# An S4D convolution with a gated MLP: inverse transform of unsummed products, a skip term on TensorE, and a tabled order of work

## The chip, the cores and the metric

One core of a Trainium2 chip. Its engines run side by side, each with a queue of its own that is worked off in order: PE (TensorE: matrix products into PSUM, with PEld its weight loads), DVE (VectorE), ACT (ScalarE), POOL (GpSimd) and SP, which here only issues DMAs. The metric is device time in microseconds (us); the kernel before took 973.34 us in the median of three runs (969.08 to 975.69). Lower is better.

## The reference, cut to what matters

```python
def A(u):                                  # L 2048, D 640, N 128
    K = 2 * einsum("dn,dnl->dl", C * dt, exp(A * dt * pos)).real
    y = irfft(rfft(K, 2 * L) * rfft(u, 2 * L))[:, :L]     # per channel
    return y + u * D_skip
def B(x):                                  # F 1728
    return (silu(x @ w1) * (x @ w3)) @ w2
sa, ca, ga, sb, cb, gb = silu(c) @ w_mod
x = x + ga * A(layernorm(x) * (1 + ca) + sa)
x = x + gb * B(layernorm(x) * (1 + cb) + sb)
```

All data is float32. A matrix product of plain float32 is two records in the trace.

## The kernel before, in words

**Stages.** The first 400 us or so compute A, the rest B (`ffn`, L1412), which the change leaves alone. A goes over five blocks of 128 channels; each block has the same steps, and steps of up to three blocks are under way at one time. Tasks have names with the block in front, and the trace has the names of the tiles:

- *Kernel chunks*, `g{b}.{c}`, eight per block (`gen_chunk` L594, `gen_tasks` L1739). POOL makes the phases (`ph`) and three products of exponentials (`z0` to `z2`, into the tiles yy and xx), ACT five sines and cosines (`s0` to `s4`, tile tr), DVE five products (`m0` to `m4`, yy and xx), PE 32 products into a PSUM tile kps (`p`, 64 records), ACT copies kps to ks (`r`), and DVE adds the skip term D_skip to one column of ks (`d`, `skip` L1761). Tiles ph, xx and yy have two buffers each; kps is one PSUM bank, used half by half.
- *h*, `h{b}.{i}`, four per block (`h_tasks` L1793): load x (`l`), normalise (`n`, four instructions, on ACT or DVE), two DVE steps (`x`, `a`; tiles hn and hb), store (`o`), and one fetch in another layout into xb (`h{b}.f`).
- *Row products*, `hh{b}.{i}` from xb and `k{b}.{i}` from ks, eight each (`first_tasks` L1812): PE (`m`, PSUM tile ps), then a copy to the spectrum sp (`e`, on ACT or DVE).
- *Spectra*, `w{b}.{i}`, eight per block (`spectra_tasks` L1851): PE makes the spectrum of h (`f`, tile fh) and of the kernel (`k`, tile fk), ACT copies the first to SBUF (`h`, tile hz). Their complex product is four real products and two sums. DVE makes two products into the tile fp (`x0`), two in place in PSUM (`x1`), and then the subtraction and the addition (`c`, two instructions of 256 elements, `both` L1879). Two such i are one *inverse* on PE (`z{b}.{j}`, `inverse` L1886, tile fz, weights wz): two products for each half of the partitions, real and imaginary part. It is copied to zt (`v0`, `v1`) and stored to zd (`o0`, `o1`).
- *Tail* (`tail_tasks` L1073): zd is read back (iz, and izb for the last block), a last set of products and an add make the new x, and its layernorm (`xn`), transposes (`tp`) and first weights lead into B.

Before all that `early_tasks` (L2000) loads x, the parameters and w_mod, makes the parameters' polar form (`pa`, `pb`, `pc`, `q`), the layernorm's statistics (`hscale`) and the modulation (`mr`, `mc`, `fold`, `cols`).

**Order.** Every step is a task of a class `Plan`: engine or two engines to choose from, a length, what it comes after, and the buffers it takes and gives. `place` (L188) walks the tasks with a model of the five engines (lengths, lags, DMA rate) and picks at each point the one that can start first, ranks breaking ties. The 1520 ranks in RANKS (L34) come from a search. The tasks are issued in that order (L270), so it is the order of every engine's queue.

Of the kernel before, what the change touches and what calls it, by code (L numbers as in the profile page):

```python
# [29 lines left out]
EXPS = ((0, 0, 0, 64.0), (0, 1, 0, 1.0), (1, 0, 0, 512.0), (1, 1, 4, 8.0), (1, 2, 0, 8.0))  # L30
# [2145 lines left out]
```

## Time and profile before

| what | value |
|---|---|
| median of three runs | 973.34 us |
| the profiled execution | 972.31 us |
| its span, first to last instruction | 970.5 us |
| mean granted TensorE clock | 0.975 |
| A, to the first product of B | 0 to 398 us |
| B | 398 to 970.5 us |

Times in the profile count from the start of the span. A group's line names line, engine, operation, output<-inputs, shape and count; then busy time, mean length in ns, and the idle time of the engine right before these instructions with what ended it. Most lines read L157, the helper through which tasks are issued, so groups go by tile names. Lengths of neighbouring DVE instructions overlap by some 0.08 us; from start to start is what the queue pays.

### The profile page before, as it was taken

Reading aid. Unit: us, or ns where it says so; the run is one execution under the profiler, and the core shown is the slowest. Engines: PE = TensorE matmul, PEld = TensorE weight load, DVE = VectorE, ACT = ScalarE, POOL = GpSimd, SP = SyncE. Lnnn points to the kernel's source line nnn. Section 1 sums busy time; section 2 is a strip of 40 time slices with the busy share of each in tenths; the row PEclk is TensorE's granted clock in tenths of the full one; section 3 lists DMA queues with packets and bytes.
Section 4 is the critical chain, followed back from the end, with each engine's and each line's share of the span. In section 5 each row is a group of like instructions: output and inputs, shape, how many; then the busy total and the mean of one; then the engine's idle time right before and its main releaser. Section 6 shows DMA issues by size and latency. Waiting matters only on the chain.

```text
span 970.5 us, 20551 instructions
## 1 busy us (share of the span) xinstructions
PE 859.9 (89%) x7985; PEld 681.8 (70%) x7985; DVE 702.0 (72%) x1395; ACT 546.4 (56%) x1022; POOL 340.5 (35%) x371
## 2 busy tenths in 40 slices
PE   1464787889899997899999999999999999999997
PEld 1132665767778884677777778888788888888775
DVE  7998899999999968886767677557456464645422
ACT  6877788979888851564434455346444344443412
POOL 1797889879799600002111111000011212120000
PEclk9996999999999999799999999999999999999999
DMA  9955453723425268935434422276342322220374
GB/s 218 275 168 191 111 136 95 177 66 106 111 80 152 74 159 206 241 118 182 122 120 139 122 96 68 82 209 194 112 134 64 102 77 86 82 82 28 108 220 133
DMA packets 110506, 127.31 MB, mean 131 GB/s; under 512 B 10568, under 2 KB 90696, under 8 KB 109128
## 3 DMA queue, kind: packets, MB, share of 16 engines
q1 hardware_dynamic: 109032, 125.21, 45.3%
q8 instruction: 63, 1.03, 0.5%
q10 hardware_dynamic: 1376, 0.79, 0.3%
q14 instruction: 35, 0.29, 0.1%
HBM read 95.82 MB, written 30.15 MB: 130 GB/s over the span
## 4 chain that ended last, share of the span: by engine, by line
PE 70%; DVE 17%; ACT 5%; issue 4%; DMA 3%; POOL 1%; SPq 1%; ACTq 0%; DVEq 0%
PE c L157 19%; PE acc L157 18%; PE X L157 12%; PE ps L157 4%; PE gu L157 3%; DVE yy L157 3%; PE kps L157 3%; PE fz L157 2%; PE fk L157 2%; DVE fp L157 2%; PE fh L157 2%; DVE hn L157 2%; DVE xx L157 2%; DVE xb L157 1%; ACT tr L157 1%
## 5 line engine op out<-in xcount | busy, mean ns | idle before, releaser
L157 PE MATMUL acc<-ah,w 128*128 128x512 f32 x560 | 173.2, 395 | 2.4 <-DMA w<-w2d 1.7
L157 PEld LDWEIGHTS acc<-ah,w 128*128 128x128 f32 x560 | 103.7, 188 | 26.4 <-issue 2.1
L157 PE MATMUL acc<-al,w 128*128 128x512 f32 x260 | 102.4, 394 | 0.0
L665 DVE TENSOR_TENSOR wl<-s,wh 128x256 fp32r<-128x256 f32 x92 | 38.9, 423 | 67.5 <-ACT wh L664 67.1
L841 POOL TENSOR_TENSOR s<-wr 128x256 f32<-128x256 f32 x22 | 16.4, 744 | 187.8 <-DMA wr<-in_w 94.8
L157 POOL TENSOR_TENSOR ph<-p,p 128x1024 int32<-128x1024 int32 x40 | 79.2, 1979 | 8.2 <-ACT tr L157 8.0
L664 ACT ACTIVATE wh<-s 128x256 fp32r<-128x256 f32 x92 | 37.6, 410 | 78.5 <-PE X L157 58.1
L157 PE MATMUL kps<-yy,xx 128*32 128x64 f32 x2560 | 51.8, 234 | 28.6 <-DVE xx L157 21.4
L157 DVE TENSOR_TENSOR yy<-yy,tr 128x512 f32<-128x512 f32 (+1 forms) x80 | 75.3, 943 | 1.2 <-ACT tr L157 0.6
L157 PEld LDWEIGHTS kps<-yy,xx 128*32 128x32 f32 x2560 | 45.1, 116 | 38.3 <-issue 22.0
L664 ACT ACTIVATE wh<-wr 128x256 fp32r<-128x256 f32 x92 | 38.4, 418 | 56.0 <-PE X L157 42.3
L842 POOL TENSOR_TENSOR s<-s,wr 128x256 f32<-128x256 f32 x22 | 16.6, 755 | 134.0 <-issue 133.9
L902 ACT ACTIVATE t<-g 128x512 f32<-128x512 f32 x44 | 27.8, 632 | 52.7 <-DVE g L866 52.7
L157 ACT ACTIVATE tr<-ph,hpi 128x512 f32<-128x512 f32 x80 | 54.6, 690 | 4.4 <-DVE xx L157 2.7
L157 PEld LDWEIGHTS acc<-al,w 128*128 128x128 f32 x260 | 48.9, 188 | 10.8 <-DVE al L665 0.3
L871 DVE SCALAR_TENSOR_TENSOR g<-t,g 128x512 f32<-128x512 f32 x48 | 33.7, 702 | 31.3 <-ACT t L902 29.3
L157 POOL TENSOR_TENSOR yy<-e,e 128x512 f32<-128x512 f32 x48 | 52.4, 1109 | 8.8 <-PE kps L157 5.9
L157 DVE TENSOR_TENSOR xx<-tr,xx 128x512 f32<-128x512 f32 x80 | 54.3, 680 | 1.1 <-ACT tr L157 1.1
L157 PE MATMUL ps<-wk,ks 128*64 128x128 f32 x640 | 42.4, 285 | 13.6 <-DVE ks L157 8.9
L157 ACT ACTIVATE tr<-ph 128x512 f32<-128x512 int32 x80 | 47.3, 598 | 12.4 <-DVE yy L157 6.5
L157 PE MATMUL ps<-wk,xb 128*64 128x128 f32 x640 | 46.1, 295 | 6.3 <-ACT sp L157 3.0
L157 PEld LDWEIGHTS ps<-wk,ks 128*64 128x64 f32 x640 | 37.0, 143 | 20.3 <-ACT hn L157 6.6
(448 smaller groups left out, 2379.7 us busy)
## 6 DMA issues: line engine op xcount, KB each, us to landing
w<-w2d SPq DMA_DIRECT2D x42, 640.0 KB, 3.9
wr<-in_w SPq DMA_DIRECT2D x50, 320.0 KB, 3.9
zd<-zt SPq DMA_DIRECT2D x40, 256.0 KB, 2.9
w2d<-w SPq DMA_DIRECT2D x14, 640.0 KB, 3.5
xs<-in_x SPq DMA_DIRECT2D x16, 320.0 KB, 11.3
hs<-hb SPq DMA_DIRECT2D x20, 256.0 KB, 2.5
xb<-hs SPq DMA_DIRECT2D x20, 256.0 KB, 4.9
iz<-zd SPq DMA_DIRECT2D x32, 160.0 KB, 5.0
```

Source lines behind the costliest of these rows:

```text
L157: self.prev = self.k.order(f(*a, **kw), self.prev)
L664: self.nc.scalar.activation(H, v, AF.Copy)
L665: eng.tensor_tensor(Lo, v, H.bitcast(F32), op=ALU.subtract)
L841: eng.tensor_tensor(s[0], u[:, 0:2], u[:, 2:4], op=ALU.add)
L842: eng.tensor_tensor(s[1], s[0], g[:, 0:2], op=ALU.subtract)
L871: V.scalar_tensor_tensor(g, th, 1.0, g, op0=ALU.add, op1=ALU.mult)
L902: tanh = lambda o, i: A.activation(o, i, AF.Tanh, scale=0.5)
```

## The change

**Unsummed products.** A constant FORM = "AABBB" gives each block a form. Blocks 2 to 4 (B) work as before. In blocks 0 and 1 (A) one DVE instruction of 1024 elements makes all four real products into an fp tile of twice the size, nothing is summed on DVE, and PE's inverse takes four products for each half in place of two, with a third set of weights (minus the first), so that PSUM makes the sums. The spectra's PSUM layout changes from (q r d) to (r q d).

**Skip term.** The DVE task `d` is gone. PE adds D_skip to kps: four products of 32x32 weights (a part of the identity) with four columns, accumulated behind the chunk's 32 products. kps becomes one tile of half a bank with one buffer.

**Third yy buffer.** In blocks 0 to 3 each third chunk takes its yy in the memory of x2[0], which is loaded later for that.

**Smaller edits.** al8, the input of the exponents, is built inside the table of exponentials. All row products of block 0 but k0.0 to k0.3 use the four rotating PSUM banks instead of three. The first two loads of zd in the tail go to the memory of a spectrum instead of a pool that opens later. Lengths of tasks are changed, which nothing reads any more.

**Order.** `place`, its model and RANKS are gone. A table ORDER of 1686 numbers gives the order: each is a task's place in the order in which tasks are added, and a tick (') means the second of its two engines. By it, among others:

- 8 of h's 20 norms are on DVE (13 before), 28 of 80 spectrum copies (20 before), 8 of 40 copies of zt (9 before).
- DVE, behind fold, up to the last add of h in block 0: h0.3.x g0.4.m0 h0.3.a g0.3.m4 g0.4.m1 h0.0.x h0.0.a h0.1.x g0.4.m2 g0.4.m3 h0.1.a g0.4.m4 h0.2.n t1.0.3 h0.2.x h0.2.a.
- DVE, from chunk 7 of block 0: g0.7.m4 h1.2.x g1.0.m0 h1.2.a g1.0.m1 hh0.0.e g1.0.m2 h1.0.x h1.0.a g1.0.m3 g1.0.m4 g1.1.m0 g1.1.m2 k0.6.e.
- PE around it: hh0.3.m hh0.7.m hh0.1.m g0.6.p hh0.5.m hh0.2.m hh0.0.m g0.7.p hh0.6.m hh0.4.m k0.7.m k0.5.m k0.6.m g1.0.p w0.0.f w0.0.k. Before: g0.7.p k0.7.m hh0.0.m g1.0.p hh0.1.m hh0.3.m hh0.2.m hh0.4.m hh0.5.m hh0.6.m hh0.7.m g1.1.p w0.0.f.
- SP: h0.f h1.1.l h1.2.l h1.0.l wb h1.1.o. Before: c1 c2 wb c3 h0.0.o h0.1.o h0.2.o c4 h0.3.o h0.f.

```diff
-RANKS = """
+ORDER = """
+1 80 78 81 79 82 83 150' 2 4 19 42 20 41 14 21 15 84 22 43 23 44 16 85 151 24 17 25 26 45 46 18 28 59 47 30 27 29 48 96 33 36 49
...
+FORM = "AABBB"
...
-    wz = np.tile(np.stack([np.block([c, s]), np.block([-s, c])], 1), (2, 1, 1))
+    wz = np.tile(np.stack([np.block([c, s]), np.block([-s, c]), np.block([-c, -s])], 1), (2, 1, 1))
...
+    def sequence(self):
...
+        for x in ORDER.split():
+            n = names[int(x.rstrip("'"))]
...
+            out.append((engs[x.endswith("'")], n))
...
+    def in_third(self, b, c):
+        return b < NB - 1 and (8 * b + c) % 3 == 2
+
+    def third(self):
+        return self.x2[0].rearrange("p j d -> p (j d)")[:, :2048].rearrange("p (r d a i) -> p r d a i", r=2, d=self.CD, a=2)
...
-        yy = w.tile([P, 2, C, 2, 32], F32, name=f"yy_{d0}", tag="yy")
+        yy = self.third() if self.in_third(d0 // P, d0 % P // C) else w.tile([P, 2, C, 2, 32], F32, name=f"yy_{d0}", tag="yy")
...
+            for q in range(4):
+                g = slice(32 * q, 32 * q + 32)
+                nc.tensor.matmul(kps.rearrange("p (e b) -> p e b", b=64)[g, :, 63], self.ident[g, g], self.dsk[g, d0 // P, d0 % P // 4:d0 % P // 4 + 4],
+                                 start=False, stop=True, skip_group_check=True, tile_position=(32 * q, 32 * q))
...
-                if b == c == 0:
-                    self.kg = self.psg.tile([P, 2, 256], F32, name="kps", tag="kg", bufs=1)
-                kps[c] = self.kg[:, c % 2]
+                kps[c] = self.psg.tile([P, 256], F32, name=f"kps{b}{c}", tag="kg", bufs=1)
...
-        def skip(c):
-            o = slice(4 * c, 4 * c + 4)
-            V.tensor_add(self.ks[b][:, o, 63], kps.pop(c).rearrange("p (e b) -> p e b", b=64)[:, :, 63], self.dsk[:, b, o])
...
-            to = k if r else prod[i // 2][:, :, i % 2 * 2:i % 2 * 2 + 2, :].rearrange("p r q d -> p q r d")
-            nc.vector.tensor_mul(to, k, bc(held[i][:, :, r], 2, 2))
+            k = bank.pop((1, i)).rearrange("p q r d -> p r (q d)")
+            h = held[i].rearrange("p q r d -> p r (q d)")
+            to = prod[i // 2][:, :, :, o, :].rearrange("p s r q d -> p s r (q d)")
+            nc.vector.tensor_mul(to, bc(k, 1, 2), bc(h, 2, 2))
...
-            for r in range(2):
+            for n, (s, r, w) in enumerate(((0, 0, 0), (0, 1, 1), (1, 1, 2), (1, 0, 1))[:2 if last else 4]):
                 for f in range(2):
                     g = slice(64 * f, 64 * f + 64)
-                    nc.tensor.matmul(bank["z", j, f], self.wz[g, r, :], p[g, r], start=(r == 0), stop=(r == 1), tile_position=(64 * f, 0))
+                    nc.tensor.matmul(bank["z", j, f], self.wz[g, w, :], p[g, s, r], start=(n == 0), stop=(n == (1 if last else 3)), tile_position=(64 * f, 0))
...
-            if b == 0:
-                x[0] = self.ks[0].rearrange("p e b -> p (e b)")[:, :1024]
...
+            x[0] = E[0][:, :, 1, :]
...
-            if u < 3:
-                z[u] = [self.ip.tile([P, 2, 512], F32, name=f"iz{u}{pr}", tag=f"iz{pr}", bufs=3) for pr in range(2)]
...
+            s = self.sp2.rearrange("p a b c -> p (a b c)")
+            t = s[:, :2048] if u == 0 else s[:, 2048:] if u == 1 else self.xb if u == 3 else self.ip.tile([P, 2048], F32, name="iz2")
```

More of the change, by code (lines that the diff above doesn't have):

```diff
@@ L28 @@
 HB2 = P // 2
[L30 removed]
+EXPS = ((0, 0, 0, 64.0), (1, 0, 0, 512.0), (1, 1, 4, 8.0), (1, 2, 0, 8.0), (0, 1, 0, 1.0))
 LOADS = 20
@@ L168 @@
 class Plan:
-    LAG = dict(PE=0.2, DVE=0.18, ACT=0.2, POOL=0.15, SP=0.0)
-    CHAIN = dict(DVE=0.12, ACT=0.12, POOL=0.07)
-    NEAR, RATE, LAND, FLY, ISSUE, AWAY, TABLE = 0.1, 235e3, 1.3, 0.7, 0.06, 8, 1.28
     def __init__(self, **rings):
@@ L258, in place @@
+        taken, done, out = {r: [] for r in self.n}, set(), []
+        for x in ORDER.split():
+            n = names[int(x.rstrip("'"))]
+            engs, _, _, after, _, _, take, give, _, _ = T[n]
+            assert n not in done and done.issuperset(after), n
+            for r, y, _ in take:
+                i = len(taken[r]) - self.n[r]
+                assert i < 0 or not uses[r, taken[r][i]], n
+                taken[r].append(y)
             for k in give:
                 uses[k] -= 1
-                given[k] = max(fin + self.LAG.get(e, 0.0), given.get(k, 0.0))
@@ L261, in place @@
-                if not uses[k]:
-                    freed[k] = given[k]
-            for m in nexts[n]:
-                left[m] -= 1
-                if not left[m]:
-                    ready.append(m)
-        assert len(end) == len(T), ("never", [n for n in T if n not in end][:20])
-        return order
-    def run(self):
-        T = self.tasks
-        found = [int(x) for x in RANKS.split()]
-        searched = [n for n in T if n not in self.own]
-        assert len(found) == len(searched)
-        self.order = self.place({n: t[4] for n, t in T.items()} | dict(zip(searched, found)))
-        for s, f, e, n in self.order:
-            if T[n][2]:
-                T[n][2](e)
+            done.add(n)
@@ L282 @@
+            out.append((engs[x.endswith("'")], n))
+        assert len(done) == len(T)
+        return out
+    def run(self):
+        for e, n in self.sequence():
+            if self.tasks[n][2]:
+                self.tasks[n][2](e)
 class K:
@@ L1113, in dst @@
                         return z[u][pr][h * 64:h * 64 + 64]
-                    load(f"iz{u}.{pr}{h}", zv[:, t0:t0 + 2, :cut], dst, 262144, done + ([f"hh{b4}.{i}.m" for i in range(8)] if u > 2 else []))
+                    load(f"iz{u}.{pr}{h}", zv[:, t0:t0 + 2, :cut], dst, 262144, done + ([f"hh{b4}.{i}.m" for i in range(8)] if u > 2 else []),
+                         "inv" if u < 2 else "change")
         def load_up(m):
@@ L1169, in lo @@
                     self.low(h[:, :k], l[:, :k], x)
-                add(f"wh{m}.{i}", "ACT", .36, hi, names + (after[i:i + 1] if after else []), rank)
-                add(f"wl{m}.{i}", "DVE", .42, lo, [f"wh{m}.{i}"], rank)
+                add(f"wh{m}.{i}", "ACT", .32, hi, names + (after[i:i + 1] if after else []), rank)
+                add(f"wl{m}.{i}", "DVE", .34, lo, [f"wh{m}.{i}"], rank)
         def down_split(m, rank):
@@ L1175, in hi @@
                 w2[m] = self.w2_high(m, w2r[m])
-            add(f"w2h{m}", "ACT", .73, hi, [f"ld{m}.{i}" for i in range(1 if m < 13 else 2)], rank, take=[("w2", 1)])
-            add(f"w2l{m}", "DVE", .82, lambda: self.w2_low(m, w2r[m], w2[m]), [f"w2h{m}"] + (["ln1"] if m in (0, 13) else []), rank)
+            add(f"w2h{m}", "ACT", .66, hi, [f"ld{m}.{i}" for i in range(1 if m < 13 else 2)], rank, take=[("w2", 1)])
+            add(f"w2l{m}", "DVE", .74, lambda: self.w2_low(m, w2r[m], w2[m]), [f"w2h{m}"] + (["ln1"] if m in (0, 13) else []), rank)
             add(f"w2k{m}", "SP", 0, lambda: self.w2_keep(m, w2[m]), [f"w2l{m}", "izb1"], rank, dma=[655360],
@@ L1237, in prepare @@
             add(f"iyb{b}", "PE", 1.9, lambda: last_inv(b), [f"izb{b}", f"lwd{b}", "border"] + (["iyb0"] if b else []), 16.0, take=[("gu", 1)])
-            add(f"iab{b}", "DVE", .7, lambda: last_plus(b), [f"iyb{b}"] + [f"lx{b}.{q}" for q in range(4)], rank, give=[("gu", f"iyb{b}"), ("w2", f"izb{b}")])
-            add(f"isb{b}", "DVE", 1.15, lambda: last_stats(b), [f"iab{b}"], rank)
+            add(f"iab{b}", "DVE", .6, lambda: last_plus(b), [f"iyb{b}"] + [f"lx{b}.{q}" for q in range(4)], rank, give=[("gu", f"iyb{b}"), ("w2", f"izb{b}")])
+            add(f"isb{b}", "DVE", .78, lambda: last_stats(b), [f"iab{b}"], rank)
             steps = {}
@@ L1267, in lo @@
                     self.low(*self.x_of(X, b, k), v[b, k])
-                add(f"tp{b}.{k}", "PE", .88, tp, [f"xn{b}.{j}" for j in range(4)] + [f"tp{b}.{k - 1}"] * (k > 0) + ([f"ia{4 + j}" for j in range(4)] + ["iab1"] if b else []), r - b)
-                add(f"v{b}.{k}", ("ACT", "DVE"), (.77, .81), shift, [f"tp{b}.{k}"], r, take=[("tmp", 1)] if k == 4 else [])
-                add(f"xh{b}.{k}", "ACT", .6, hi, [f"v{b}.{k}"], r)
-                add(f"xl{b}.{k}", "DVE", .69, lo, [f"xh{b}.{k}"], r, give=[("tmp", f"v{b}.{k}")] if k == 4 else [])
+                add(f"tp{b}.{k}", "PE", .6, tp, [f"xn{b}.{j}" for j in range(4)] + [f"tp{b}.{k - 1}"] * (k > 0) + ([f"ia{4 + j}" for j in range(4)] + ["iab1"] if b else []), r - b)
+                add(f"v{b}.{k}", ("ACT", "DVE"), (.7, .74), shift, [f"tp{b}.{k}"], r, take=[("tmp", 1)] if k == 4 else [])
+                add(f"xh{b}.{k}", "ACT", .54, hi, [f"v{b}.{k}"], r)
+                add(f"xl{b}.{k}", "DVE", .6, lo, [f"xh{b}.{k}"], r, give=[("tmp", f"v{b}.{k}")] if k == 4 else [])
         prepare(0, 16)
@@ L1587, in inv @@
             self.sp2 = self.fpool.tile([P, 16, P, 2], F32, name="sp2")
-        plan.add("inv", None, 0, inv, ["cols", "mag1"], 0)
+        plan.add("inv", None, 0, inv, ["cols", "mag1", "hscalef", "colsf", "q0.v1", "q1.v1"] + [f"h0.{i}.a" for i in range(4)] + [f"k0.{i}.e" for i in range(4)] +
+                 [f"rw{g}" for g in range(4)], 0)
         self.early_tasks(e)
@@ L1613, in border @@
             self.x2 += [self.fp.tile([P, 4, D], F32, name=f"x2{i}") for i in (2, 3)]
-        plan.add("change", None, 0, change, [f"g{b}.7.p", f"g{b}.7.d"] + [f"h{b}.{i}.x" for i in range(4)], 0, own=True)
+        plan.add("change", None, 0, change, [f"g{b}.7.p", f"g{b}.7.r"] + [f"h{b}.{i}.x" for i in range(4)], 0, own=True)
         self.tail_tasks(border, cut)
@@ L1787, in gen_tasks @@
                     give=[("tr", n + f"s{(0, 0, 1, 3, 4)[i]}")])
-            add(n + "p", "PE", 1.1, lambda c=c: ch[c][4](), [n + f"m{i}" for i in range(5)], t + 3,
-                take=[("kg", 1)], give=[("yy", n + "z0"), ("xx", n + "z2")])
+            add(n + "p", "PE", 1.3, lambda c=c: ch[c][4](), [n + f"m{i}" for i in range(5)] + (["dsk"] if b == 0 else []), t + 3,
+                take=[("kg", 1)], give=[(yy, n + "z0"), ("xx", n + "z2")])
             add(n + "r", "ACT", .27, lambda c=c: rows(c), [n + "p"] + ([f"k{b - 1}.{i}.m" for i in range(8)] if b else ["exp0", "q0.t0", "q1.t0"]), t + 3, give=[("kg", n + "p")])
-            add(n + "d", "DVE", .1, lambda c=c: skip(c), [n + "r"] + (["dsk"] if b == 0 else []), t + 3, give=[("kg", n + "p")])
     def h_tasks(self, b):
@@ L1803, in h_tasks @@
             place = (lambda: self.pbank("hn")) if b else (lambda: self.psg.tile([P, 512], F32, name="hn", tag="f", bufs=3))
-            add(n + "n", ("ACT", "DVE"), (1.95, .85), lambda e, i=i, place=place: self.h_norm(b, i, place(), e), [n + "l", "hscale"], t, take=[(bank, 1)],
+            add(n + "n", ("ACT", "DVE"), (1.89, 1.66), lambda e, i=i, place=place: self.h_norm(b, i, place(), e), [n + "l", "hscale"], t, take=[(bank, 1)],
                 give=[("xq", n + "l")] if b else [])
@@ L1925, in spectra_tasks @@
             j = i // 2
+            y = "c" if last else "x"
             n = f"z{b}.{j}."
-            add(n + "z", "PE", 1.95, lambda j=j: inverse(j), [f"w{b}.{i - 1}.c", f"w{b}.{i}.c"], t + W["late"], take=[("bank", 1), ("bank", 1, "'")],
-                give=[("fp", f"w{b}.{i - 1}.x0")])
+            add(n + "z", "PE", 1.92 if last else 3.86, lambda j=j: inverse(j), [f"w{b}.{i - 1}.{y}", f"w{b}.{i}.{y}"], t + W["late"], take=[("bank", 1), ("bank", 1, "'")],
+                give=[("fp", f"w{b}.{i - 1}.x")])
             for f in range(2):
@@ L1951, in exps @@
                 A.activation(E[t][:, :, m, :], x[0][:, :, k:k + n], AF.Exp, scale=-s)
-        add(f"al8{b}", ("POOL", "DVE"), (1.9, 1.13), begin, [f"al{min(b, 1)}"] + (["inv"] if b > 1 else []) + ([f"exp{b - 1}"] if b > 1 else ["turn1"] if b else []), t, port=True,
-            take=[("xs", 1)] if b == 1 else [])
-        add(f"exp{b}", "ACT", 3.46, exps, [f"al8{b}"] + ([f"g{b - 2}.7.z{i}" for i in range(3)] if b > 1 else ["turn1"] if b else []), t, table="exp",
-            give=[("xs", f"al8{b}")] if b == 1 else [])
+        add(f"al8{b}", ("POOL", "DVE"), (1.9, 1.13), begin, [f"al{min(b, 1)}"] + ([f"exp{b - 1}"] + [f"g{b - 2}.{c}.z{i}" for c in (5, 6, 7) for i in range(3)] if b > 1 else ["turn1"] if b else []), t, port=True)
+        add(f"exp{b}", "ACT", 3.46, exps, [f"al8{b}"], t, table="exp")
         add(f"mag{b}", ("POOL", "DVE"), (1.07, .62), lambda e: self.eng(e).tensor_tensor(E[1][:, :, 0], E[1][:, :, 0], bc(self.mag[:, b], 2, 4), op=ALU.mult),
@@ L2071, in early_tasks @@
             for j in range(4):
-                add(f"su{b}{j}", "ACT", .85, lambda b=b, j=j: st[b][0](j), [f"x{b}"], t + .01 * j)
-                add(f"sq{b}{j}", "ACT", .9, lambda b=b, j=j: st[b][2](j), [f"mean{b}"], t + .05 + .01 * j, give=[("xs", f"x{b}")])
+                add(f"su{b}{j}", "ACT", .74, lambda b=b, j=j: st[b][0](j), [f"x{b}"], t + .01 * j)
+                add(f"sq{b}{j}", "ACT", .83, lambda b=b, j=j: st[b][2](j), [f"mean{b}"], t + .05 + .01 * j, give=[("xs", f"x{b}")])
             add(f"mean{b}", "DVE", .1, lambda b=b: st[b][1](), [f"su{b}{j}" for j in range(4)], t, port=True)
@@ L2086, in scale @@
             self.h_rs = self.rsqrt(self.gp, self.h_ss, NJ, "h", (self.h_nm, 1.0), 1.0 / D, [t[:, i * NJ:(i + 1) * NJ] for i in range(2)])
-        add("hscale", "DVE", 6.5, scale, [f"mean{b}" for b in range(4)] + [f"sq{b}{j}" for b in range(4) if b not in W["stat_v"] for j in range(4)], W["stat"](4), take=[("f2", 1)])
+        add("hscale", "DVE", 5.5, scale, [f"mean{b}" for b in range(4)] + [f"sq{b}{j}" for b in range(4) if b not in W["stat_v"] for j in range(4)], W["stat"](4), take=[("f2", 1)])
         add("hscalef", None, 0, None, ["hscale"], give=[("f2", "hscale")])
@@ L2095, in rows_begin @@
             A.activation(m[:96, 384:], pm[0][:96, 384:], AF.Copy)
-        add("m", "ACT", .9, rows_begin, ["mr4"], 20, take=[("hz", 4)])
+        add("m", "ACT", .6, rows_begin, ["mr4"], 20, take=[("hz", 4)])
         pr = {}
@@ L2111, in early_tasks @@
             add(f"pr{g}", "PE", .9, lambda g=g: spread(g), ["m"], 21, take=[("f2", 1)], give=[("hz", "m")])
-            add(f"rw{g}", "ACT", .8, lambda g=g: keep(g), [f"pr{g}", "lat1", "pa4"], 21, give=[("f2", f"pr{g}")])
+            add(f"rw{g}", "ACT", .55, lambda g=g: keep(g), [f"pr{g}", "lat1", "pa4"], 21, give=[("f2", f"pr{g}")])
         def fold():
@@ L2117, in fold @@
             V.tensor_mul(self.rB, self.rB, self.rows[2])
-        add("fold", "DVE", 1.6, fold, [f"rw{g}" for g in range(4)], 22, port=True)
+        add("fold", "DVE", 3.2, fold, [f"rw{g}" for g in range(4)], 22, port=True)
         add("wb", "SP", 0, lambda: nc.sync.dma_start(self.wb, self.t_wb), ["fold", "mr4", "lat1", "turn1"], 60, dma=[2097152])
```

183 lines of the change are left out of this document (73 added, 110 removed), and 101 rows, old and new, of tables (ORDER, RANKS).

## The prediction

> **What bounds the kernel now.** I read the profile's page first, then the table by stages, then the order of time on PE and DVE where stages meet.
>
> ```profile
> span 970.5 us, 20551 instructions
> PE 859.9 (89%) x7985; PEld 681.8 (70%) x7985; DVE 702.0 (72%) x1395; ACT 546.4 (56%) x1022; POOL 340.5 (35%) x371
> ```
>
> These averages hide the stages. Below: stretch, its length, busy time (instructions) of PE, weight loads, DVE, ACT, POOL, granted clock, DMA share, GB/s.
>
> ```profile
> 34.00:62.00 28.00, 19.53 (x255) 9.72 (x256) 27.19 (x43) 22.80 (x46) 27.39 (x25) 1.00 0.87 257
> 62.00:92.00 30.00, 10.41 (x202) 6.86 (x201) 29.13 (x53) 20.54 (x36) 26.01 (x25) 0.72 0.39 142
> 92.00:124.00 32.00, 24.37 (x540) 20.50 (x542) 26.73 (x52) 24.48 (x42) 23.89 (x25) 0.89 0.54 136
> 124.00:170.00 46.00, 35.47 (x648) 27.14 (x646) 45.06 (x87) 39.75 (x70) 44.06 (x46) 0.96 0.44 113
> 170.00:211.00 41.00, 31.93 (x710) 29.80 (x712) 39.19 (x76) 34.64 (x57) 34.54 (x34) 0.96 0.49 124
> 211.00:260.00 49.00, 44.82 (x891) 36.64 (x883) 45.86 (x81) 44.07 (x74) 41.85 (x39) 0.97 0.48 123
> 260.00:310.00 50.00, 47.64 (x1039) 40.46 (x1036) 48.14 (x89) 41.30 (x73) 47.70 (x50) 1.00 0.42 113
> 310.00:350.00 40.00, 39.89 (x836) 33.24 (x838) 33.74 (x65) 30.45 (x57) 22.10 (x19) 1.00 0.23 65
> 350.00:376.00 26.00, 24.83 (x298) 18.19 (x296) 20.98 (x46) 8.47 (x16) 0.00 (x0) 1.00 0.88 222
> 376.00:398.00 22.00, 13.92 (x79) 8.87 (x76) 19.45 (x76) 6.47 (x10) 0.63 (x1) 0.72 0.91 215
> 398.00:970.50 572.50, 560.78 (x2501) 446.96 (x2499) 339.73 (x668) 249.38 (x498) 65.82 (x88) 1.00 0.39 120
> ```
>
> Up to 211, DVE is all but full (45.06 of 46, 39.19 of 41) and PE is not (35.47 and 31.93). From 211 to 376 it turns: PE is busy 44.82 + 47.64 + 39.89 + 24.83 = 157.2 of 165 us. From 398 on the gated MLP keeps PE at 560.78 of 572.5, and the change does not reach it. So whatever is gained is gained before 376, by giving PE its work earlier; work that is added to PE is not free.
>
> **The change part by part.** I read the new table by name: a number is a place in the list of tasks, a tick means the task's second engine. Durations are of the profiled execution, 972.31 us (span 970.5 and 1.81 around it); the median of three runs is 973.34.
>
> *1. DVE relief.* DVE's groups, with count, busy time, mean ns and idle time before them:
>
> ```profile
> L157 DVE TENSOR_TENSOR yy<-yy,tr 128x1024 f32<-128x1024 f32 x40 | 48.4, 1210 | 0.9 <-ACT tr L157 0.6
> L157 DVE TENSOR_TENSOR fp<-fp,fk 128x256 f32<-128x256 f32 x80 | 29.7, 411 | 0.2
> L157 DVE TENSOR_TENSOR fk<-fk,hz 128x512 f32<-128x512 f32 x40 | 27.6, 691 | 0.0
> L157 DVE TENSOR_TENSOR fp<-fk,hz 128x512 f32<-128x512 f32 x40 | 27.3, 683 | 3.8 <-PE fk L157 2.7 <-ACT hz L157 0.8
> L157 DVE TENSOR_SCALAR hn<-xq,rs_y_h,rs_n_h 128x128 f32<-128x128 f32 x44 | 18.1, 412 | 1.2
> L157 DVE COPY sp<-ps 128x512 f32<-128x512 f32 x20 | 13.4, 683 | 3.2 <-PE ps L157 3.1
> L157 DVE TENSOR_TENSOR ks<-kps,dsk 128x4 f32<-128x4 f32 x40 | 6.0, 157 | 9.8 <-ACT ks L157 5.6 <-PE kps L157 3.1 <-ACT hn L157 1.1
> ```
>
> Blocks 0 and 1 lose 32 of the 80 sums: 32 x 29.7 / 80 = 11.9 us. Their two products of 512 become one of 1024, 1.21 (nearest row, the same size, also from PSUM) for 0.69 + 0.68: 16 x 0.16 = 2.6. The 40 skip adds go: 6.0, and up to 9.8 of waits in front of them. The table puts 8 norms on DVE for 13 (52 instructions, 44 of them in the row above): 5 x 4 x 0.41 = 8.2 less; it puts 28 spectrum copies on DVE for 20, 8 x 0.6 = 4.8 more. DVE loses 24 us or so. None of it shortens the span by itself after 211; up to 211 it can.
>
> *2. Where the first Spectra product starts.* Starts, lengths, what ran:
>
> ```profile
> 71.00 1.20 DVE L157 TENSOR_TENSOR yy<-yy,tr 128x1024 f32<-128x1024 f32 x1
> 72.13 0.68 DVE L157 TENSOR_TENSOR xx<-tr,xx 128x512 f32<-128x512 f32 x1
> 72.73 0.68 DVE L157 TENSOR_TENSOR hn<-hn,rw 128x512 f32<-128x512 f32 x1
> ...
> 95.39 0.68 DVE L157 TENSOR_TENSOR hb<-hn,rw 128x512 f32<-128x512 f32 x1
> ```
> ```profile
> 105.54 1.85 PE L157 MATMUL kps<-yy,xx 128*32 128x64 f32 x64 [0.99 <-DVE xx L157]
> 108.09 1.59 PE L157 MATMUL ps<-wk,ks 128*64 128x128 f32 x16 [0.69 <-DVE ks L157]
> 109.51 1.20 PE L157 MATMUL ps<-wk,xb 128*64 128x128 f32 x16
> ...
> 123.72 1.13 PE L157 MATMUL fh<-sp,wb 128*64 128x128 f32 x16
> ```
>
> Today h of block 0 is ready late (its last add, hb, at 95.39), so its eight row products (ps from xb) all stand behind chunk 7's product (kps at 105.54, the eighth) and end just ahead of fh at 123.72. Behind fold 32 DVE tasks stand ahead of h's last add; the new table puts 16 there, and six of the eight row products ahead of chunk 7. What then holds fh is the last of block 0's copies, k0.6, on DVE: behind chunk 7's last product stand twelve instructions of 512 (0.60 from start to start, 72.13 to 72.73) and one of 1024 (1.13, 71.00 to 72.13): 8.3 us. Chunk 7's last product itself I leave at 105.5: the DVE tasks ahead of it come to 1 us more by these lengths, against skip adds and waits that are gone. So fh starts at about 114: 10 us earlier.
>
> One load has to keep up: the 2 MB of wb move on SP's queue from 71 to behind three loads of block 1's x, the third of which waits for a buffer that the DVE norm of h1.1 frees, 4.8 us ahead of chunk 7's last product, at some 100.5.
>
> ```profile
> 71.07 0.33 SPq L157 DMA_DIRECT2D wb<-in_t_wb  x1
> ```
> ```profile
> wb<-in_t_wb SPq DMA_DIRECT2D x1, 2048.0 KB, 8.9
> ```
>
> Then 4 issues and wb, 2 us, and 8.9 to landing: 111.5. It hides with 2.5 us to spare; if that cover is gone, fh waits for it one for one.
>
> *3. PE's added work.* From the chain of work, start and length:
>
> ```profile
> 319.37 1.92 PE fz L157 x8
> 321.29 1.06 PE fk L157 x16
> 322.35 1.82 PE fh L157 x32
> ...
> 332.13 1.10 PE kps L157 x61
> ```
> ```profile
> L157 PEld LDWEIGHTS kps<-yy,xx x2560: 106/110/178, 46.4 to 346.1; 128*32 128x32 f32 x197
> L157 PE MATMUL kps<-yy,xx x2560: 216/219/317, 46.4 to 346.2; 128*32 128x64 f32 x197
> ```
>
> Eight inverses of blocks 0 and 1 take 8 matmuls for 4 (16 records for 8): 8 x 1.92 = 15.4 us. The skip term is four 32x32 products (8 records) per chunk. Below: records alone, 1.10 / 64 = 0.017 each, 0.14 us. Above: eight weight loads one after another, 8 x 0.110, and a change of array layout, seen as fk's 1.06 behind fz against 1.82 / 2 = 0.91 behind fh, 0.15: 1.03. I take 0.14 + 0.15 = 0.29, near the lower end, since neighbouring kps records do overlap. 31 chunks stand behind fh (30 today): 31 x 0.29 = 9.0, and one kps more, 1.1.
>
> The rule against this step is in the Trainium skill's "TensorEngine Tiling (Array Packing)", section "Key Properties": a change of tiling mode drains the engine. The rows show 0.15 for one kind of change; with a drain as long as one load and one matmul (0.11 + 0.22) twice a chunk, the sum would be 31 x 0.51 = 16 us more.
>
> *4. PE from fh to the last inverse.* Busy 124 to 376 is 35.47 + 31.93 + 157.2 = 224.6. With 15.4 + 9.0 + 1.1 it is 250.1; at full clock instead of 0.96 up to 211, 67.4 x 0.04 = 2.7 less: 247.4. PE's idle share is 4.7% in 211 to 376 (7.8 of 165) and 0.3% in 310 to 350. I take 2.5%, between them, as DVE has some 24 us less to do: 253.7. The inverse of the last block then ends at 114 + 253.7 = 367.7 where it is 376 now: 8.3 us earlier.
>
> *5. Edits with one answer.* The third yy buffer lets POOL run ahead; the wait that it shortens (total, times, longest) is
>
> ```profile
> POOL yy L157 <- PE kps L157: 14.9, 11, 3.9
> ```
>
> and POOL, at 22.10 of 40 from 310 on, ends before PE does: 0 by itself. With one buffer for kps in place of two halves, a chunk's product waits for ACT's copy of the chunk before: 40 products between 46.4 and 346.2 are 7.7 us apart in the mean, 0. The exponents' input (al8), built in place, waits for more readers; that is POOL's work too, 0. First loads of z moved ahead: the rows of z never end last in the tail; what does is
>
> ```profile
> 376.30 3.14 DMA zd<-zt
> ...
> 380.31 4.67 DMA izb<-zd
> ```
>
> which depends on the last inverse only. 0, between -2 and +1.
>
> Sum: 972.31 - 8.3 = 964.0, 1.0% below the median; 1% is about what a measurement of this kernel can tell from no change (three runs spread over 969.08 to 975.69).
>
> **The rivals.** *Better:* PE is as unbroken as in 310 to 350 (0.3%: 248.1) and chunk 7 comes 4 us earlier, by the skip adds' waits and a clock above the 0.72 of 62 to 92: 110 + 248.1 = 358.1, 954.4 us. For it: DVE, full up to 211, has the most to lose. Against: four queues in an order fixed ahead meet on the chip as they come.
>
> *Gain eaten:* PE's idle share stays at 4.7% (259.6) and wb or ACT brings fh only at 117: 376.6, 973 us. For it: in 211 to 310 all four engines are over 85% busy (PE 92.5, DVE 94.0, ACT 85.4, POOL 89.6 of 99), so each can be the one that holds the others.
>
> *Slower, ACT takes DVE's place:* in 124 to 211 ACT is busy 74.4 of 87 and is handed five norms. If PE keeps the 77.4% of that stretch through blocks 0 and 1, then 67.4 + 15.4 + 14 x 0.29 - 2.7 = 84.2 take 108.8 and end at 222.8 instead of 211; with 6.0 more behind (17 x 0.29 + 1.1) the last inverse is 17.8 late, 990 us. It decides (over 983.1) where PE is busy under 83% there; at 92.5% nothing is gained. Against: DVE, not ACT, was full.
>
> *Slower, skip products not overlapped:* 1.03 a chunk, 31 x 0.74 = 22.9 more: 987. It decides from 0.91 a chunk. For it: a layout that no row shows. Against: the 0.017 of a kps record. (The drain of the Trainium skill's rule in part 3 would give 980; it shares this chance.)
>
> **How the numbers follow.** Forecast (958 to 968) 0.40; better (946 to 958) 0.18; eaten (968 to 981) 0.25; ACT 0.11; skip products 0.06. Faster by over 1%, below 963.6: 0.18 and 0.24 of the forecast's 0.40. Slower by over 1%, above 983.1: 0.17. Within: 0.41. The range 951 to 983 leaves out about 0.06 below and 0.13 above. The forecast's own range is 958 to 968.
>
> **What would show it.** Right: fh first at 112 to 116; inverse rows of 3.8 in blocks 0 and 1; chunk products of 1.3 to 1.5; PE over 95% busy from there to the last inverse at 363 to 372; DVE below 90%; the tail of 22 us and the MLP's 572.5 unchanged. Wrong: fh waiting for wb; PE waiting for ACT's copies; chunk products near 2; a tail that is bound by a load.

## The result, and the profile after

The changed kernel takes 957.94 us (median of 4 runs, 955.41 to 960.15), the kernel before 972.66 (4 runs): the ratio is 0.9841 with a 95% interval of 0.9813 to 0.987. The profiled execution took 955.41 us where the one before took 972.31, so the two profiles show 16.9 us between them and the medians 14.7.

The head of the page after:

```profile
span 953.6 us, 21224 instructions
PE 869.9 (91%) x8369; PEld 688.7 (72%) x8369; DVE 683.9 (72%) x1293; ACT 550.9 (58%) x1036; POOL 342.3 (36%) x371
```

The same table by stages as before (stretch, length, PE, weight loads, DVE, ACT, POOL, granted clock, DMA share, GB/s):

```profile
62.00:92.00 30.00, 18.96 (x283) 13.01 (x286) 24.03 (x49) 27.35 (x48) 28.34 (x29) 0.77 0.73 202
92.00:124.00 32.00, 30.17 (x686) 25.98 (x688) 31.43 (x46) 30.47 (x56) 30.61 (x31) 1.00 0.38 118
124.00:170.00 46.00, 41.37 (x818) 32.06 (x816) 42.46 (x68) 43.23 (x73) 40.31 (x41) 1.00 0.60 153
170.00:211.00 41.00, 40.78 (x880) 34.07 (x877) 38.70 (x53) 37.31 (x68) 38.60 (x39) 1.00 0.36 96
211.00:260.00 49.00, 47.73 (x946) 39.15 (x944) 45.64 (x75) 40.98 (x69) 44.83 (x45) 1.00 0.34 89
260.00:310.00 50.00, 49.72 (x1116) 41.56 (x1115) 45.96 (x78) 42.77 (x75) 44.41 (x43) 1.00 0.38 97
```

PE fills where it stood idle: 30.17 of 32 us from 92 to 124 (24.37 before) and 40.78 of 41 from 170 to 211 (31.93). The granted clock is 1.00 in every stretch from 92 to 310; it was 0.89 to 0.97 from 92 to 260.

Where Spectra begins, on PE (start, length):

```profile
102.53 1.16 PE L151 MATMUL kps<-yy,xx 128*32 128x64 f32 x64 [0.19 <-DVE xx L151]
103.62 0.24 PE L151 MATMUL kps<-dsk,ident 32*32 32x4 f32 x8
...
109.75 1.17 PE L151 MATMUL kps<-x,xx 128*32 128x64 f32 x64
110.85 0.24 PE L151 MATMUL kps<-dsk,ident 32*32 32x4 f32 x8
111.02 1.14 PE L151 MATMUL fh<-sp,wb 128*64 128x128 f32 x16
...
119.98 3.70 PE L151 MATMUL fz<-fp,wz 64*128 64x512 f32 x16
123.61 1.13 PE L151 MATMUL fh<-sp,wb 128*64 128x128 f32 x16
```

Chunk 7's product starts at 102.53 (105.54 before), fh at 111.02 (123.72). An unsummed inverse takes 3.63 us from its start to that of the product behind it (123.61 - 119.98) where a summed one took 1.92. The skip term's eight records hold PE for 0.17 us (111.02 - 110.85).

The stretch from the first fh to the end of the last inverse, before and after, in the columns of the table:

```profile
123.72:375.18 251.46, 224.05 (x4394) 185.47 (x4392) 232.56 (x437) 198.25 (x342) 190.37 (x185) 0.98 0.46 121
```
```profile
111.02:356.18 245.16, 237.08 (x4774) 191.95 (x4768) 223.04 (x354) 203.12 (x352) 192.71 (x185) 1.00 0.48 122
```

PE does 13.0 us more and is idle for 8.1 us instead of 27.4. So the last inverse ends 19.0 us earlier: 12.7 from the start, 6.3 from the stretch. Behind it 953.6 - 356.18 = 597.4 us are left (595.3 before), which gives 2.1 back. In all 14 profiles of this study that remainder lies between 595.3 and 597.8: whatever differs, differs ahead of the last inverse.

### The profile page after: what moved, and what is told of

It reads as the page before. It is cut to its first block, busy times and chain, and to the rows that moved or that the text cites. A ratio compares the mean times of both kernels' runs of the same rounds, so it can differ in the third digit from the quotient of the medians.

```text
span 953.6 us, 21224 instructions
## 1 busy us (share of the span) xinstructions
PE 869.9 (91%) x8369; PEld 688.7 (72%) x8369; DVE 683.9 (72%) x1293; ACT 550.9 (58%) x1036; POOL 342.3 (36%) x371
## 3 DMA queue, kind: packets, MB, share of 16 engines
q1 hardware_dynamic: 109032, 125.27, 45.8%
## 4 chain that ended last, share of the span: by engine, by line
PE 73%; DMA 9%; ACT 7%; DVE 5%; POOL 3%; issue 2%; SPq 1%; ACTq 0%; DVEq 0%; POOLq 0%
PE c L151 19%; PE acc L151 18%; PE X L151 12%; PE ps L151 5%; PE kps L151 4%; PE fz L151 4%; PE gu L151 3%; PE fk L151 3%; PE fh L151 3%; DMA xs<-in_x 2%; PE iy L151 1%; DMA sp<-zd 1%; ACT tr L151 1%; DVE yy L151 1%; DMA dsk<-in_d_skip 1%
## 5 line engine op out<-in xcount | busy, mean ns | idle before, releaser
L151 DVE TENSOR_TENSOR yy<-yy,tr 128x512 f32<-128x512 f32 (+1 forms) x60 | 56.7, 946 | 3.1 <-ACT tr L151 2.3
L151 PE MATMUL kps<-yy,xx 128*32 128x64 f32 x1920 | 37.8, 231 | 19.0 <-DVE xx L151 14.8
L151 PE MATMUL fz<-fp,wz 64*128 64x512 f32 x224 | 54.2, 608 | 0.3 <-DVE fp L151 0.3
L151 PEld LDWEIGHTS kps<-yy,xx 128*32 128x32 f32 x1920 | 32.7, 115 | 27.6 <-issue 11.4
L599 DVE TENSOR_TENSOR wl<-wr,wh 128x256 fp32r<-128x256 f32 x92 | 40.3, 438 | 14.8 <-ACT wh L598 14.7
L598 ACT ACTIVATE ah<-h 128x512 fp32r<-128x512 f32 x26 | 16.4, 632 | 53.1 <-PE acc L151 53.1
```

Source lines behind the costliest of these rows:

```text
L151: self.prev = self.k.order(f(*a, **kw), self.prev)
L598: self.nc.scalar.activation(H, v, AF.Copy)
L599: eng.tensor_tensor(Lo, v, H.bitcast(F32), op=ALU.subtract)
```

## The experiments

Four things in the change can carry the gain: the order, the unsummed products, the skip term on PE, the third yy buffer. The theory is that of the prediction, taken further: the order brings fh forward, the relief of DVE keeps PE unbroken, PE's added work is paid one for one, and the third buffer is worth nothing by itself. The rivals: one part alone does it, or PE is not the bound. Each run is timed beside the kernel before, whose median in these rounds was 971.93 to 973.71; "ratio" is to that, with its 95% interval. Differences below are of medians, so 1 or 2 us between two kernels say little. "To fh" is the time from the first kps product to the first fh (loads bring the first product anywhere from 45.8 to 49.0), "fh to end" that from there to the end of the last inverse.

| kernel | median us | ratio | to fh | fh to end |
|---|---|---|---|---|
| before | 972.66 | 1 | 77.3 | 251.5 |
| after | 957.94 | 0.9841 (0.9813 to 0.987) | 63.7 | 245.2 |
| e1_old_order | 993.78 | 1.0207 (1.0174 to 1.024) | 83.1 | 268.2 |
| e2_sum_on_dve | 967.58 | 0.9938 (0.9917 to 0.9959) | 62.9 | 255.5 |
| e3_skip_on_dve | 981.12 | 1.0084 (1.0054 to 1.0113) | 77.2 | 254.8 |
| e4_two_yy | 974.78 | 1.002 (1.0002 to 1.0039) | 67.4 | 259.9 |
| e5_skip_later | 975.79 | 1.0029 (1.0008 to 1.0051) | 70.3 | 258.4 |
| e6_no_skip | 957.89 | 0.9838 (0.9808 to 0.9867) | 65.8 | 247.3 |
| e7_abbbb | 961.53 | 0.9878 (0.9851 to 0.9904) | 62.8 | 251.9 |
| e8_before_third | 970.40 | 0.9983 (0.9961 to 1.0005) | 74.7 | 253.3 |
| e9_old_order_sums | 989.67 | 1.0153 (1.0117 to 1.019) | 82.0 | 263.8 |
| e10_all_back | 999.79 | 1.0273 (1.024 to 1.0306) | 70.8 | 280.3 |
| e11_aaabb | 962.99 | 0.99 (0.9861 to 0.994) | 64.1 | 250.4 |
| e12_idle_adds | 966.38 | 0.9919 (0.9887 to 0.9951) | 64.9 | 253.5 |

**The sums back on DVE, in both blocks and in block 1 alone.** In the task of the product:

```diff
-FORM = "AABBB"
+FORM = "BBBBB"     (e7: "ABBBB")
+        joined = b < 2 and last
...
                     nc.vector.tensor_mul(k if r else ..., k, bc(held[i][:, :, r], 2, 2))
+                if joined:
+                    both(i)
```

> The changed kernel and its order, but the partial products of blocks 0 and 1 are summed on DVE right behind the product, and the inverse of these blocks takes 4 matmuls again: DVE +14.5 us, PE -15.4 us. DVE is busy 31.43 + 42.46 + 38.70 = 112.6 of 119 us from 92 to 211. Theory (DVE is the bound there if it does the sums): 127 us of DVE work in 119, so 6 to 10 us longer up to 211, 963 to 969 us; PE's busy share there falls below 90%. Rival (PE is the bound, the sums would hide on DVE): the last inverse 8 to 15 us earlier, 943 to 950 us. Between them: the two cancel, 955 to 961.

> The changed kernel and its order with the partial products of block 1 alone summed on DVE, right behind the product: PE -7.7 us, DVE +7.2 us, between 170 and 260. Theory (DVE, which gains nothing from PE's relief, is the bound wherever it does the sums): half of the 9.6 us that both blocks cost, 961 to 964 us. Rival (only block 0 is short of DVE; at block 1 PE is the bound with 40.78 of 41 us): 950 to 956 us.

Measured: 9.6 us and 3.6 us more than after. The start of fh does not move; the stretch behind it grows, though PE has less to do. Blocks 0 and 1 of e2 by stages:

```profile
124.00:170.00 46.00, 37.10 (x704) 30.04 (x704) 44.91 (x80) 41.56 (x70) 37.27 (x39) 0.93 0.51 131
170.00:211.00 41.00, 35.37 (x816) 30.44 (x816) 39.53 (x69) 35.00 (x62) 36.52 (x37) 1.00 0.39 102
```

DVE is full again (44.91 of 46) and PE falls to 37.10 and 35.37. So the unsummed form is worth about 10 us here, and its worth comes from DVE alone: PE does 13.7 us more for it (8 inverses of 3.63 us for 1.92). Both theories came as put down.

**Block 2 unsummed too.** `FORM = "AAABB"`, the place of its sums left empty.

> The changed kernel and its order with block 2's partial products unsummed too: PE +7.7 us, DVE -7.2 us, between 240 and 300. Theory (behind 211 PE is busy 47.73 of 49 and 49.72 of 50 and DVE has some 3 us to spare in each stage, so PE pays in full): 962 to 966 us. Rival (DVE still sets the pace there, as the sums of block 1 did when they were put back): 953 to 958 us.

Measured: 5.1 us more, as the theory had it: in block 2 DVE's relief no longer pays for PE's work. In this run PE is busy for all of the 50 us from 260 to 310, and DVE for 41.06. With none, one, two and three blocks unsummed the time is 967.6, 961.5, 957.9 and 963.0: the change has the best of the four.

**The skip term.** e3 takes the four products out and adds on DVE right behind ACT's copy; e5 delays that add by six DVE tasks and gives kps its two halves again; e6 leaves the term out.

```diff
-            for q in range(4):
-                g = slice(32 * q, 32 * q + 32)
-                nc.tensor.matmul(kps...[g, :, 63], self.ident[g, g], self.dsk[g, ...], tile_position=(32 * q, 32 * q))
...
+            V.tensor_add(self.ks[b][:, o, 63], v[:, :, 63], self.dsk[:, b, o])     (e3; e5: six DVE tasks later; e6: nothing)
```

> The changed kernel and its order, but the skip term is added on DVE again, right behind ACT's copy of the chunk's product; the four 32x32 products go. PE -5.3 us behind fh (31 x 0.17) by the trace, DVE +6.3 us and waits for PE and ACT at its head (9.8 us in the kernel before). Theory (DVE's waits at the head of its queue cost more than the products): 959 to 966 us. Rival (PE-bound from 124 on, DVE has room): 952 to 955 us.

> The changed kernel with the skip term on DVE once more, but with the add six DVE tasks behind ACT's copy (or ahead of its first reader, if that comes sooner), and kps in two halves as in the kernel before, so that neither DVE nor the next product has to wait for it. Theory 1 (the 23 us of the run with the add right behind the copy were DVE standing at the head of its queue for ACT, up to 6.9 us at a time): most of it goes, 956 to 965 us, DVE's wait for ACT's ks below 8 us. Rival 1 (a skip term on DVE costs by itself, wherever it stands): 972 us or more. Rival 2 (PE is the bound, its 31 x 0.17 us count): 951 to 955 us.

> The changed kernel and its order without the skip term (the four 32x32 products of each chunk are left out and nothing stands in for them, so the D term is missing from the output). Theory (PE is nearly unbroken from the first fh on): 31 x 0.17 = 5.3 us less, 952 to 954 us. Rival 1 (the products cost PE more than their starts show, by the change of array layout): 8 to 30 us less. Rival 2 (other engines set the pace): 957 to 959 us, PE's idle share up by the 5 us.

Measured: 23.2 and 17.9 us more, and no change without the term. Both expectations of e3 were too low. In e3 the order lets ACT's copy stand behind a table load and five exponentials, and DVE behind that copy; ACT first, then DVE:

```profile
79.15 1.28 ACT L151 ACT_TABLE_LOAD   x1
80.45 3.70 ACT L151 ACTIVATE late<-late 128x1024 f32<-128x1024 f32 x5
84.06 0.37 ACT L151 ACTIVATE ks<-kps 128x256 f32<-128x256 f32 x1
```
```profile
84.45 0.17 DVE L151 TENSOR_TENSOR ks<-kps,dsk 128x4 f32<-128x4 f32 x1 [6.87 <-ACT ks L151]
```

Up to 400 us DVE waits for ACT's ks for 29.8 us in e3 and for 5.0 in e5. Yet the delay of e5 takes only 5.3 of the 23.2 us away, not most of them: its theory 1 fell, and its first rival came. What is left shows in its waits up to 400 us (who waits for whom, total, times, longest):

```profile
POOL xx L151 <- PE kps L151: 20.5, 12, 6.0
PE ps L151 <- DVE ks L151: 11.1, 10, 2.7
DVE ks L151 <- PE kps L151: 7.7, 6, 2.5
ACT ks L151 <- DVE ks L151: 6.4, 4, 3.2
```

The row products wait for the add, the add for the product, and POOL for the product as well (6.9 us in all after). A term of 0.16 us on DVE thus closes a round PE, ACT, DVE, PE, in which each hop enters a nearly full queue. No run takes the hops of this round apart.

e6 overturned a premise of the prediction. 31 x 0.17 = 5.3 us of PE work went, and the time stayed. Its stretch:

```profile
114.29:361.62 247.33, 235.01 (x4522) 189.13 (x4520) 223.04 (x354) 202.59 (x353) 192.87 (x185) 0.99 0.48 122
```

PE is busy 2.1 us less than after and idle 4.2 us more (12.3 for 8.1). Some of that idle time is spread: this profile is of the slowest of its four executions, 959.13, and that of after of the fastest, 955.41. The medians decide, 957.89 and 957.94: at 96.7% busy PE is not the bound in the sense that taking this work off it helps.

**Idle adds on DVE.** After, with an add of two operands in SBUF (the memory beside PSUM) in the place of e3's:

```diff
+            V.tensor_add(self.pad[:, :4], self.dsk[:, b, o], self.dsk[:, b, o])
```

> The changed kernel, skip term on PE and all, with 40 more DVE adds of the same size (128x4) at the place where the add stood in the first of the two runs with the skip term on DVE; they read the D values alone, write a place that nobody reads, and wait for nothing. Theory (the skip term on DVE cost 18 to 23 us by the round from PE over ACT and DVE back to PE, not by DVE's time): 957 to 961 us. Rival (DVE is full, and 40 instructions more are what it cost): 968 us or more.

Measured: 8.4 us more, between the two, because the adds were not what they were meant to be. Their group, then two places of them on DVE:

```profile
L151 DVE TENSOR_TENSOR pad<-dsk 128x4 f32<-128x4 f32 x40 | 21.8, 545 | 0.0
```
```profile
256.65 2.11 DVE L151 TENSOR_TENSOR pad<-dsk 128x4 f32<-128x4 f32 x2
...
317.30 0.15 DVE L151 TENSOR_TENSOR pad<-dsk 128x4 f32<-128x4 f32 x1
```

and POOL at the first of them:

```profile
255.76 1.07 POOL L151 TENSOR_TENSOR xx<-late 128x512 f32<-128x512 f32 x1 [0.35 <-PE kps L151]
256.78 1.96 POOL L151 TENSOR_TENSOR ph<-p,p 128x1024 int32<-128x1024 int32 x1
```

They took 21.8 us, not 6.3: the two at 256.65 end at 258.76 with POOL's instruction (258.74), the one at 317.30, where POOL waits, takes 0.15. The other places agree: of the 25 rows of 0.20 us or more, 20 end at most 0.05 us behind the end of a POOL instruction. So 21.8 us of DVE that wait for no data cost 8.4 us, about 0.4 each. At that rate the 6.4 us of adds in e5 (40 x 0.160) are worth some 2.5 of its 17.9 us. This is an estimate, which takes it that the loss grows with DVE's time; by it the waits are the larger part.

**The third yy buffer, in the new order and in the old.** e4: `in_third` returns False, the order on every engine unchanged. e8: the kernel before with `third()` for every third chunk of blocks 0 to 2. (In e8 the buffer's last use overwrites x values of the first output rows, which are loaded early there; those rows change.)

> The changed kernel and its order on every engine, with two yy buffers and not three: what changes is that POOL's first size of a chunk waits for the product two chunks back instead of three. Theory (as predicted: the third buffer is worth nothing by itself): 957 to 960 us, the waits of POOL for kps up by less than 10 us. Rival (POOL, busy 28.34 of 30 and 30.61 of 32 from 62 to 124, sets chunk 7, and the buffer is what lets it): fh later by 3 to 8 us, 961 to 967 us.

> The kernel before, its operations and its order, with one thing of the change: every third chunk of blocks 0 to 2 uses the third yy buffer. POOL's 14.9 us of waits for kps in front of yy shrink. Theory (the third buffer is worth what the order lets it be; in the old order POOL comes early enough): 968 to 973 us. Rival (the buffer alone is worth the 16.8 us that its loss costs the changed kernel): 956 to 961 us.

Measured: 16.8 us more without it in the new order; 1.5 us less with it in the old one, which its interval (to 1.0005) does not tell from nothing, although POOL's 14.9 us of waits for kps in front of yy fall to 0.6 there. The same waits up to 400 us, e4 and then after:

```profile
POOL yy L151 <- PE kps L151: 29.1, 13, 4.9
```
```profile
POOL yy L151 <- PE kps L151: 3.7, 1, 3.7
```

Both expectations of e4 fell short: the rival's later fh came (115.5 for 111.0), but its time, 961 to 967 us, did not. Most of the loss is behind fh, 259.9 us for 245.2. The order puts POOL's products of exponentials for the third chunk ahead of the PE product that frees a second buffer, so each such place is a wait on an engine that is nearly full (30.61 of 32 us from 92 to 124).

**The order.** e1: the operations after, in the order of the kernel before (a task goes later only where what it needs isn't there yet). e9: the same with the sums on DVE in their old places. e10: the new order with the sums on DVE, the skip term as in e5, and two yy.

> The changed kernel, every operation as it is there, in the order of the kernel before (same sequence on each engine; where a buffer of the changed kernel isn't free yet, a task waits for its turn). Theory (the order brings the first Spectra product forward, the relief of DVE keeps PE unbroken behind it, and each is worth little without the other): the first fh falls back from 111 to 119-124, PE carries 15.4 + 5.3 us more behind it, 970 to 982 us. Rival 1 (the relief of DVE does it, the order only follows): fh stays below 115 and the time within 958 to 964. Rival 2 (the third yy buffer does it, which is still here): POOL runs ahead, fh below 117, 960 to 966.

> The run in the old order once more, now with the partial products of blocks 0 and 1 summed on DVE as a step of its own, at the place that the sums have in the kernel before: what is left of the change is the skip term on PE, the third yy buffer, the single kps buffer and the exponents' input in place. Theory (in the old order the 15.4 us of added inverses come out in full, since PE has no work brought forward, and the skip term on PE is worth little): 975 to 982 us. Rival 1 (the skip term on PE is worth its 18 us in any order): 955 to 962 us. Rival 2 (the single kps buffer and the input in place are what costs 21 us there): 988 us or more.

> The new order with the old operations: the sums of blocks 0 and 1 on DVE behind the product, the skip term on DVE six tasks behind the copy, two yy buffers. Theory (each part bears on the same loop of PE, ACT, DVE and POOL, and the losses of 9.6, 18 and 17 us add up): 995 to 1006 us, worse than the kernel before; the order is only good for these operations. Rival (the three losses are one and the same slip of the schedule, so that the worst of them covers the others): 976 to 984 us.

Measured: 20.6 and 16.0 us above the kernel before for e1 and e9. e10 is 41.9 us above after, and 26.1 above the kernel before: with these old operations the new order is a loss. The losses of e2, e5 and e4 (9.6 + 17.9 + 16.8 = 44.3) add up to nearly that of e10, as its theory had it. In e10 the new order alone brings fh to 70.8 us behind the first product, against 77.3 before and 63.7 after: about half of the 13.6 us. But then PE is starved:

```profile
118.81:399.06 280.25, 230.89 (x4458) 189.30 (x4456) 238.75 (x434) 204.25 (x352) 194.19 (x186) 0.95 0.42 107
```

e1 and e9 are no clean test of the operations, since the old order makes two waits of its own with them. The row products of block 0 now need the room that opens behind the modulation's column factors (`cols`, from tile pv), and stand behind it: fh is 4.7 us (e9) and 5.1 us (e1) later than before. And the x rows loaded on SP share their room with the third buffer; SP, then DVE, of e9:

```profile
276.98 0.37 SPq L149 DMA_DIRECT2D zd<-zt  x1
289.43 2.56 SPq L149 DMA_DIRECT2D x<-in_x  x4
292.09 2.14 SPq L149 DMA_DIRECT2D zd<-zt  x3
```
```profile
299.36 0.69 DVE L149 COPY zt<-fz 128x512 f32<-128x512 f32 x1 [7.26 <-issue]
```

The load waits on its queue until 289.43, the z stores behind it, and DVE's next copy for a zt buffer: 7.26 us. (The profile names no releaser of that wait; the stores land 7.3 us, median, behind their issue, which fits it.) Up to 12 of e9's 16 us are these two; the other 4, between the 32x32 products, the single kps buffer and the exponents' input in place, stay open. e9's time is in the range of its second rival, but by the number only, as the parts that this rival names can have no more than those 4 us. e1, with fh at 128.9, lies beyond all that was expected of it. An old order without the two waits was not tried, nor one laid out anew for the old operations with three yy buffers.

## Why the prediction was right, and where it was not

The direction and the range held; the size did not. The forecast of 964.0 was 8.6 us above the profiled execution after, 6.1 above the median: a gain of 8.7 us on the median of 972.66 was forecast, and 14.7 came. The median after, 957.94, lies just under the forecast's own 958 to 968. Two terms of the sum were too large, the time of chunk 7 and PE's added work (parts 2 and 3). The third yy buffer, put at 0, and the skip term on PE are worth far more in this order than was said (part 5); the sum holds their worth unseen, in the idle time that it chose for PE (part 4).

*1. DVE relief.* Right. DVE's groups after:

```profile
L151 DVE TENSOR_TENSOR fp<-fk,hz 128x1024 f32<-128x1024 f32 x16 | 19.5, 1218 | 1.4 <-PE fk L151 1.1 <-ACT hz L151 0.3
L151 DVE COPY sp<-ps 128x512 f32<-128x512 f32 x28 | 18.9, 683 | 2.9 <-PE ps L151 2.8
L151 DVE TENSOR_TENSOR fp<-fp,fk 128x256 f32<-128x256 f32 x48 | 17.9, 416 | 0.5
L151 DVE TENSOR_TENSOR fk<-fk,hz 128x512 f32<-128x512 f32 x24 | 16.6, 690 | 0.0
L151 DVE TENSOR_TENSOR fp<-fk,hz 128x512 f32<-128x512 f32 x24 | 16.5, 689 | 8.9 <-PE fk L151 7.5 <-ACT zt L151 0.9 <-ACT wh_u L151 0.3
```

Sums 11.8 us less (11.9 predicted), products 27.6 + 27.3 - 52.6 = 2.3 (2.6), copies 5.5 more (4.8). DVE's total fell by 18.1 us (702.0 to 683.9), not 24; the rest is spread over many small groups and was not traced. That it counts up to 211 was right too: e2 and e7 price it at 9.6 and 3.6 us.

*2. The first fh.* The mechanism was right, a term too large. DVE at this place:

```profile
101.71 0.68 DVE L151 TENSOR_TENSOR xx<-tr,xx 128x512 f32<-128x512 f32 x1
...
110.15 0.68 DVE L151 COPY sp<-ps 128x512 f32<-128x512 f32 x1
```

Block 0's last copy ends 0.2 us ahead of fh, and it starts 8.4 us behind chunk 7's last product (8.3 predicted). wb held nothing. What was left at 105.5, chunk 7 itself, came at 102.5: 3.0 us. What brought it forward is not shown. From the first product to chunk 7's it is 59.1 us before and 55.2 after, 58.0 with the skip adds back (e5) and 58.9 without the third buffer (e4); but it is 57.4 in e6 as well, which has neither skip adds nor two buffers, so some 2 us of this have another reason, which was not traced. The rest of e5's later fh (6.6 us in all) stands behind chunk 7, where row products wait for the add.

*3. PE's added work.* Too dear. The inverses cost 8 x 1.71 = 13.7 us (15.4 predicted), the skip products 5.3 (9.0), the one product more 1.1: 20.1. PE's busy time rose by 13.0 only, as the work that was there before went faster by 7: the granted clock of the stretch rose from 0.98 to 1.00, by an estimate 224 x 0.02 = 4.5 us; the other 2.6 are not traced. I had taken 2.7 for the clock. A skip term took 0.17 us per chunk, far from the bound of 1.03, and by e6 none of it is in the time. The Trainium skill's "TensorEngine Tiling (Array Packing)", section "Key Properties", says that a change of tiling mode drains the engine. A drain as long as the prediction took it, 16 us in all, does not show here.

*4. PE from fh to the last inverse.* 253.7 predicted, 245.2 measured: busy 237.1 for 247.4, idle 3.3% for 2.5%. The sum was of the right form. That its 2.5% came so near was luck in part: the reason given was DVE's relief alone, and in e4, with all of that relief but two yy buffers, PE is idle for 19.0 of the 259.9 us, 7.3%. The premise that "work that is added to PE is not free" failed for most of the work added: 5.3 us of skip products taken off PE changed nothing (e6, to some 4 us by the two intervals), and 13.7 us of inverses taken off in blocks 0 and 1 at DVE's cost lost 9.6 (e2). PE's full table is the outcome of a schedule in which DVE, ACT and POOL hand it work in time, not proof that it sets the pace. In block 2, where DVE has room, 6.8 us more on PE (4 x 1.71) did cost 5.1 (e11).

*5. Edits with one answer.* This step failed for the third yy buffer. The third yy buffer was put at 0 "by itself", from POOL's 14.9 us of waits in the old order; e8 bears that out, and it is the wrong question, since the new order is laid out on three. There it is worth 16.8 us. Likewise the skip term was priced by its instructions and DVE's waits for them (6.0 and 9.8 on DVE, 9.0 on PE); to take it off DVE is worth about 18 us in this order, of which by the estimate above some 15 are the round of waits. The single kps buffer and the moved z loads were not tested apart; behind the last inverse 2.1 us were lost for the 0 (-2 to +1) of the prediction, inside the spread of all profiles.

The sum of it: the last inverse at 356.2 for 367.7, of which 3.0 are chunk 7, 10.3 PE's busy time, less 1.8 of idle time. (The prediction counted the gain from an end of the last inverse at 376; it was at 375.2, so its sum was 0.8 us too kind there.)

*The rivals.* The better case, at 954.4, is the one that came, at 955.4, by its earlier chunk 7 (3 us of its 4) and PE's lesser work, not by an unbroken PE (0.3% idle there, 3.3% here); so that its number fits is luck. ACT did become the fullest engine in one stage (43.23 of 46 from 124 to 170), but PE was busy there for 41.37 us, 90%, and for 94% of 124 to 211 (82.15 of 87), over the 83% at which that rival decided. The skip products overlapped.

Of what was to show it: the inverses' rows of 3.70 (3.8), chunk products of 1.27 (1.3 to 1.5) and PE busy for 96.7% held, or nearly; fh at 111.0 came ahead of 112 to 116, and the last inverse at 356.2 well ahead of 363 to 372; DVE was at 91.0%, not below 90.

## What to carry to other kernels

In a loop over several engines with an order fixed ahead, price an edit by the hops and buffers that it takes out of the round, not by its instructions; and price it in the order that it comes with, since three parts worth 44 us together in the new order, one of which is worth nothing in the old, give 15 us over the kernel before, and the new order without the three loses 26 (e10). An engine at 97% is shown to be a bound only when taking work off it shortens the time: one kernel with some work left out tells. The same engine can be no bound in one block and the bound in the next (e2, e11). A buffer that borrows the room of a load ties that load's queue, and all that stands behind it there, to the buffer's last reader.

## What the runs showed of the hardware

Four 32x32 products (8 records) right behind 128x32 ones held PE for 0.17 us from start to start (110.85 to 111.02), with no gap ahead of fh. An add of 128x4 took 0.157 us on DVE with one operand in PSUM (mean of 40, before), and 0.146 to 1.894 us (median 0.312) with both in SBUF (e12); the long ones end with an instruction of POOL, the one shown that began while POOL waited took 0.15. The Trainium skill's "GPSIMD Engine Reference", section "Specifications", lists the SBUF interfaces as shared with VectorE, with contention for DVE instructions with two SBUF inputs. These rows agree, and give it a size.
